# Pairs in long runs and in blocks, and a convolution in products and sums, in a routed-attention and gated-FFN kernel

## The chip, the cores and the metric

One core of a Trainium2 chip runs the whole program. The metric is device time in microseconds; each kernel is run several times and the median counts.

## The reference

Attention in which a query sees only the keys that fall to the same one of 16 centroids, then a gated FFN with a convolution over three tokens:

```python
# q, k, v: (4, 8, 768, 64) float32, centroids: (8, 16, 64)
q_assign = argmax(q_n . c_n), k_assign = argmax(k_n . c_n)      # per head, by normalized vectors
scores = where(q_assign == k_assign, q @ k.T / 8, -1e9)
attn_out = softmax(scores) @ v
x = attn_out as (4, 768, 512)
h = relu(x @ w_in)                                              # (4, 768, 1024)
conv = w[0]*h[t-1] + w[1]*h[t] + w[2]*h[t+1]                    # per channel, zero at both ends
out = (h * sigmoid(conv)) @ w_out                               # (4, 768, 512) float32
```

## The kernel before, in words

The work on attention goes by 16 pairs of heads g, four to a batch. A pair's q and k are loaded into one buffer `qk_in` (three of them, `NQK`), turned so that the head dimension lies on the partitions, cast to f16 into `ext`, and compared with the centroids (`assign`, L329; `argmax`, L356, steps M0 to M6). The centroid of each token becomes three rows that stand below the 64 rows of q and k in `ext`, so that a score is one matmul with 67 rows (`scores`, L435, step S), followed by one exponential (`exps`, L449, step E) and the product with v (`values`, L459, step V). A slot t is one pair with either its first 512 queries or its last 256; there are 32 slots with 3 or 6 steps of each kind, 144 in all.

Pairs 0 to 7 are loaded a head at a time (`load_q`, `load_k`, L268 to L274, steps LQ and LK: 768 runs of 256 bytes each) and turned by fp32 transposes on TensorE (`transposes`, L289, step T) with a copy out of PSUM (`chunk_copy`, L312, step Q). Pairs 8 to 15, named in `BLOCKS`, are loaded in quarters (`load_blocks`, L276, step LZ: 768 runs of 128 bytes each) and turned in 32x32 blocks on VectorE (`turn_blocks`, L302, step Z). For all pairs but the first, the second head is moved to the lower partitions by a copy within SBUF (`shift_pair`, L322, step CX) and the three rows are written by a transfer (`bias_rows`, L405, step BX). v is loaded by LV and cast by CV, the FFN's weights by LW and CW.

The output of attention is normalized (`reciprocals`, `normalize`, steps P and N) into `x16` and turned into `xT`, either by transposes on TensorE with a copy (`x_transposes`, `xT_copy`, steps X and Y) or by a transposing transfer (`xT_transfer`, L506, step XD).

The FFN goes by 24 units n, six to a batch: four units with two blocks of 128 channels for the first 510 tokens, two units with four blocks for the last 258. A unit is two steps of the first layer (`ffn_in`, L528, step I, 4 matmuls of 512 columns or 8 of 256), a relu into `hpad` (`relu`, L543, step R) which has columns for the neighbours on both sides, the convolution, a tanh (`tanh`, L589, step H) and the gate (`gate`, L599, step G), which writes `hg`. The second layer is `ffn_out` (L614, step O, two matmuls of 512 columns), then a copy and a store (`evac`, `store`, steps F and FX).

The convolution of 21 units is made on VectorE by `tap` (L565): per block one product of the middle tap with its weight (L572), which starts at an even column of `hpad`, and two fused products and sums (L574, steps b and c beside a). That of units 19, 22 and 23 is made on TensorE by `conv` (L576, step W, three matmuls with diagonal matrices of weights that GpSimd prepares in 24 steps `_tp`, L750), and its tanh and gate go block by block.

The order is written out by hand: `PLAN` (L26) is one list of steps, and each step issues its instructions on the engines that it names. So the order within each engine, and within SP's queue, which issues nearly all transfers, is that of the list. A transfer that waits for its data holds all that stand behind it in that queue.

## Time and profile before

| | before |
|---|---|
| time, median of 3 runs | 251.25 us |
| lowest and highest | 248.7 and 251.94 us |
| span of the profiled execution | 247.8 us, 6354 instructions |
| TensorE, VectorE, ScalarE, GpSimd busy | 229.4, 212.1, 210.1, 77.8 us |
| data moved | 35.40 MB in 97254 packets, 87537 of them under 512 bytes |

The profile is of one execution and is told by its span, from the first to the last instruction; the time of a run is taken around that and is 0.9 to 4.1 us longer. The clock that was granted to TensorE was full in all stretches but one. Busy times of groups on TensorE overlap where matmuls follow each other without a gap; the chain of waits counts each stretch once.

### The profile page before, as it was taken

To read this page: it belongs to the slowest core of one execution; us is meant where nothing else is said; L and a number is where in the kernel's file an instruction comes from. 1 tells how busy PE (TensorE), PEld (TensorE's weight loads), DVE (VectorE), ACT (ScalarE), POOL (GpSimd) and SP (SyncE) were. 2 spreads that over 40 slices of the span, in tenths; PEclk is the share of its full clock that TensorE was granted. 3 is DMA by queue.
4 is the path that set the end of the run, shared out by engine and by line. 5 is a ranking of instruction groups with operands and counts; after the bars stand their busy time and mean duration, and the time that the engine had idled before them with its cause. 6 is when DMAs were issued, how large, how long until landed. Compare 5 with 4: busy or idle time off the path is not lost.

```text
span 247.8 us, 6354 instructions
## 1 busy us (share of the span) xinstructions
PE 229.4 (93%) x2443; PEld 146.2 (59%) x2443; DVE 212.1 (86%) x484; ACT 210.1 (85%) x277; POOL 77.8 (31%) x135
## 2 busy tenths in 40 slices
PE   8698889999898699969998999999999999999994
PEld 4465556557554466745465648764657677564661
DVE  4888775899999889976999999999999997899640
ACT  5586889998998699986998999998999999974442
POOL 3312352524265100462212011540365000449600
PEclk9999999999999999997999999999999999999999
DMA  6998979998779999999987961421207022111223
GB/s 147 269 247 136 221 236 289 374 264 139 140 156 164 125 131 159 118 210 197 138 161 170 172 193 55 99 57 32 70 15 224 3 66 65 42 45 54 107 96 127
DMA packets 97254, 35.40 MB, mean 143 GB/s; under 512 B 87537, under 2 KB 91657, under 8 KB 97225
## 3 DMA queue, kind: packets, MB, share of 16 engines
q1 hardware_dynamic: 97081, 34.97, 65.1%
q8 instruction: 19, 0.31, 0.6%
q14 instruction: 10, 0.08, 0.1%
q10 hardware_dynamic: 144, 0.03, 0.1%
HBM read 23.11 MB, written 6.29 MB: 119 GB/s over the span
## 4 chain that ended last, share of the span: by engine, by line
PE 38%; DVE 23%; ACT 16%; DMA 15%; issue 4%; SPq 3%; DVEq 0%; ACTq 0%
ACT attn L454 10%; DVE cnv L574 9%; PE flex L534 9%; PE sc L440 8%; PE flex L617 7%; DMA qk_in<-in_k_dram 5%; PE sc L617 4%; PE flex L467 4%; DMA xT<-x 3%; DVE hg L605 3%; DMA ext<-spk 3%; DMA ext<-ext 2%; DMA qk_in<-in_q_dram 2%; DVE x L490 2%; PE flex L295 2%
## 5 line engine op out<-in xcount | busy, mean ns | idle before, releaser
L454 ACT ACTIVATE attn<-sc 128x1024 f16<-128x1024 f32 x144 | 141.6, 1039 | 8.0 <-PE sc L440 7.6
L440 PE MATMUL sc<-ext 67*128 67x256 f16 (+1 forms) x384 | 83.9, 328 | 2.8 <-DMA ext<-spk 1.5
L574 DVE SCALAR_TENSOR_TENSOR cnv<-hpad,cwcol,cnv 128x510 f16<-128x510 f16 (+1 forms) x108 | 68.9, 658 | 0.5
L467 PEld LDWEIGHTS <-attn 128*128 128x128 f16 x1152 | 46.3, 97 | 14.5 <-ACT attn L454 2.9
L534 PE MATMUL flex<-xT,w_in 128*128 128x512 f16 (+1 forms) x248 | 48.7, 332 | 3.8 <-DMA xT<-x 2.4
L467 PE MATMUL flex<-v,attn 128*128 128x65 f16 x1152 | 50.5, 193 | 0.2
L440 PEld LDWEIGHTS <-ext 67*128 67x128 f16 x384 | 37.4, 113 | 21.9 <-issue 6.3
L310 POOL CAST ext<-qkT 128x768 f16<-128x768 f32 (+1 forms) x31 | 29.2, 960 | 52.9 <-PE sc L440 30.1
L617 PE MATMUL flex<-w_out,hg 128*128 128x512 f16 x144 | 38.7, 378 | 0.0
L534 PEld LDWEIGHTS <-w_in 128*128 128x128 f16 x256 | 24.7, 98 | 21.2 <-issue 6.4
L605 DVE SCALAR_TENSOR_TENSOR hg<-th,hpad 128x1020 f16<-128x1020 f32 (+3 forms) x31 | 30.4, 997 | 1.2 <-ACT th L597 1.2
L617 PEld LDWEIGHTS <-hg 128*128 128x128 f16 x192 | 17.7, 97 | 17.3 <-issue 0.6
L548 ACT ACTIVATE hpad<-flex 128x512 f16<-128x512 f32 x39 | 23.1, 608 | 5.3 <-PE flex L534 4.6
L597 ACT ACTIVATE th<-cnv 128x1020 f32<-128x1020 f16 (+1 forms) x21 | 22.5, 1073 | 3.0 <-DVE cnv L574 2.7
L557 POOL COPY hf<-hpad 128x6 f16<-128x6 f16 x16 | 5.7, 360 | 56.6 <-ACT hpad L548 51.7
L750 POOL TENSOR_SCALAR taps<-id,cwcol 128x128 f16<-128x128 f16 x24 | 21.2, 899 | 0.0
L490 DVE TENSOR_TENSOR x<-flex,rec 128x256 f16<-128x256 f32 x48 | 19.7, 415 | 0.5
L310 POOL CAST v<-v_in 128x768 f16<-128x768 f32 x13 | 12.4, 955 | 22.2 <-DMA v_in<-in_v_dram 14.1
L304 DVE STREAM_TRANSPOSE qkT<-qk_in 128x384 f32<-128x384 f32 x32 | 16.8, 552 | 2.5 <-DMA qk_in<-in_k_dram 2.2
L572 DVE TENSOR_SCALAR cnv<-hpad,cwcol 128x510 f16<-128x510 f16 (+1 forms) x54 | 17.4, 344 | 1.7 <-ACT hpad L548 1.5
L295 PE MATMUL flex<-id,qk_in 128*128 128x128 f32 x96 | 14.9, 281 | 2.4 <-ACT qkT L308 0.7
L337 PE MATMUL flex<-qkT,cP 128*32 128x192 f32 x240 | 12.9, 332 | 1.9 <-DVE x L490 1.2
(86 smaller groups left out, 190.1 us busy)
## 6 DMA issues: line engine op xcount, KB each, us to landing
v_in<-in_v_dram SPq DMA_DIRECT2D x16, 384.0 KB
out_dram<-o_sb SPq DMA_DIRECT2D x24, 256.0 KB
qk_in<-in_q_dram SPq DMA_DIRECT2D x16, 192.0 KB
qk_in<-in_k_dram SPq DMA_DIRECT2D x16, 192.0 KB
qk_in<-in_q_dram SPq DMA_DIRECT2D x32, 96.0 KB
qk_in<-in_k_dram SPq DMA_DIRECT2D x32, 96.0 KB
ext<-ext SPq DMA_DIRECT2D x15, 192.0 KB
hg<-in_moe_w_in_dram SPq DMA_DIRECT2D x4, 512.0 KB
```

Source lines behind the costliest of these rows:

```text
L310: (nc.vector if name == "d" else nc.gpsimd).tensor_copy(out=to, in_=src)
L440: nc.tensor.matmul(to[:, m], lhsT=keys[:, kt], rhs=ext_b[g % NE][0:KR, h, 0, Q0[a] : Q0[a] + QN[a]], start=True, stop=True, skip_group_che ...
L454: nc.scalar.activation(to, sc[at].rearrange("p n s -> p (n s)"), AF.Exp, scale=0.125)
L467: nc.tensor.matmul(avp(at)[:, jq + (2 * h if a else 0), 0 : D + 1], lhsT=attn[t, i // 3][:, o : o + P], rhs=v16_b[g % NE][:, h, kt, 0 : D ...
L490: nc.vector.tensor_tensor(out=to, in0=src, in1=by, op=ALU.mult)
L534: nc.tensor.matmul(bank[at][:, QN[a] * f : QN[a] * (f + 1)], lhsT=w_in16[:, r, f0 + (a + 1) * p + f, :], rhs=xT[:, b % 2, r, Q0[a] : Q0[a] ...
L548: nc.scalar.activation(to, src, AF.Relu)
L574: nc.vector.scalar_tensor_tensor(out=cnv, in0=src, scalar=w, in1=cnv, op0=ALU.mult, op1=ALU.add)
L597: nc.scalar.activation(to, pre, AF.Tanh, scale=0.5)
L605: nc.vector.scalar_tensor_tensor(out=hg_b[b][:, f0 + fs.start : f0 + fs.stop, LO[a] : LO[a] + N], in0=rows_of(th_t[n], n)[:, fs], scalar=1 ...
L617: nc.tensor.matmul(bank[at][:, 0:Dm], lhsT=hg_b[b][:, fb, P * tq : P * (tq + 1)], rhs=w_out16[:, fb, :], start=(fb == 0), stop=(fb == NFB ...
L750: nc.gpsimd.tensor_scalar(out=taps16[:, fb, kk, :], in0=id16[:], scalar1=cwcol[:, fb, kk : kk + 1], scalar2=None, op0=ALU.mult)
```

## The change

The first four pairs (`SPLIT`) are loaded in long runs: k in 1536 bytes per partition, q in 1024 and 512. The tokens of these pairs then stand in another order in `ext`, and the copies, the casts, `assign`, the scores, the tiles of v and the relu of the first batch follow that order with strides. For pairs 1 to 3 one cast writes both heads' first halves, and the copy within SBUF moves half of each head. Pairs 6 and 7 join the blocks, ten in all. `qk_in` gets a fourth buffer. The convolution of all 24 units is made on VectorE, with three products per block and two sums per unit; the one on TensorE, its 24 diagonal matrices, and tanh and gate by block are gone. The x tiles of slots 4 to 7 go through TensorE. `PLAN` is new from end to end. The number of steps that differ:

| step | before | after |
|---|---|---|
| LQ + LK, whole or long loads | 32 | 23 |
| LZ, block loads; Z, block turns | 64; 32 | 80; 40 |
| T (transposes in them) | 25 (96) | 19 (72) |
| W, convolution on TensorE; _tp | 10; 24 | 0; 0 |
| plain products; fused; sums | 54; 108; 0 | 192; 0; 48 |
| H, tanh; G, gate | 31; 31 | 24; 24 |
| X, x tiles by TensorE; XD, by transfer | 8; 24 | 12; 20 |
| between the 12th and the 87th E: I, O, T | 23, 20, 10 | 18, 8, 2 |
| there: LZ, LQ + LK, LV + LW, XD | 64, 10, 17, 12 | 72, 0, 17, 8 |

The core of the diff (both lists cut to their first and last lines):

```diff
-NQK = 3
+NQK = 4
...
-BLOCKS = (8, 9, 10, 11, 12, 13, 14, 15)
+NPD = 2
+BLOCKS = (6, 7, 8, 9, 10, 11, 12, 13, 14, 15)
+SPLIT = (0, 1, 2, 3)
 
 PLAN = (
-    "_id LQ.0.0 _cent _zero _cT _k.0@0 _v.0 _v.3 _n0 _pk.3 LK.0.0 _k.1@0 _id16 _v.4 _io _k.2@0 _cw0 _pk.1 "
...
-    "O.3.5.3@2 O.3.3.0@6 FX.3.4 Fa.3.5 O.3.3.1@6 O.3.3.2@6 FX.3.5 O.3.3.3@6 Fa.3.3 FX.3.3 "
+    "_cent LK.0.0 _zero _cT _v.1 _k.0@0 _n0 _id _k.1@0 LQ.1.0 _k.2@0 _k.3@0 _k.4@0 _k.5@0 LQ.0.0.0 _k.6@0 "
...
+    "O.3.3.3@1 FX.3.5 Fa.3.3 FX.3.3 "
 )
...
+    JP = (4, J - 4)
+    JH = J // 2
...
-    def qk_part(g, x, h):
-
-        t = qk_in(g)
-        return t[:, h, :, x] if g < NBH else t[:, x, :, h]
-
-    def load_q(g, h, queue=nc.sync):
+    def load_q(g, part, h=None):
         b, h0 = batch_pair(g)
-        queue.dma_start(qk_part(g, 0, h), q[b, h0 + h].rearrange("(j p) d -> p j d", p=P))
-
-    def load_k(g, h, queue=nc.sync):
+        t = qk_in(g)[:, 0]
+        if g in SPLIT:
+            hs = heads(h)
+            j0, n = JP[0] * part, JP[part]
+            to = t.rearrange("p (h j) d -> p h (j d)", h=2)[:, hs, D * j0 : D * (j0 + n)]
+            src = q[b, h0 + hs.start : h0 + hs.stop, P * j0 : P * (j0 + n)]
+            nc.sync.dma_start(to, src.rearrange("h (p j) d -> p h (j d)", j=n))
+        else:
+            to = t.rearrange("p (j h) d -> p j h d", h=2)[:, :, part]
+            nc.sync.dma_start(to, q[b, h0 + part].rearrange("(j p) d -> p j d", p=P))
+
+    def load_k(g, h=None):
         b, h0 = batch_pair(g)
-        queue.dma_start(qk_part(g, 1, h), k[b, h0 + h].rearrange("(p j) d -> p j d", j=J))
+        t = qk_in(g)[:, 1]
+        if g in SPLIT:
+            hs = heads(h)
+            to = t.rearrange("p (h j) d -> p h (j d)", h=2)[:, hs]
+            src = k[b, h0 + hs.start : h0 + hs.stop]
+            nc.sync.dma_start(to, src.rearrange("h (p j) d -> p h (j d)", j=J))
+        else:
+            to = t.rearrange("p (j h) d -> p j h d", h=2)[:, :, h]
+            nc.sync.dma_start(to, k[b, h0 + h].rearrange("(p j) d -> p j d", j=J))
 
...
     def transposes(g, c, at):
         chunk_at[g, c] = at
-        n = 3 if g < NBH else 4
-        for i in range(n):
-            x, j = divmod(n * c + i, J)
-            blocks = qk_t[g][:, x, j].rearrange("p n d -> p (n d)")
-            nc.tensor.transpose(bank[at][:, P * i : P * (i + 1)], blocks, id128[:])
+        t = qk_t[g]
+        if g < NBH:
+            blocks = [(c % 2, J * (c // 2) + 2 * i) for i in range(JH)]
+        elif g in SPLIT:
+            blocks = [(x, J * h + 2 * i) for x in range(2) for h in range(2) for i in range(JH)]
+            blocks = [y for y in blocks if (2 if y[1] % J == 4 else y[0]) == c]
+        else:
+            blocks = [divmod(4 * c + i, J) for i in range(4)]
+            blocks = [(x, 2 * j) for x, j in blocks]
+        for i, (x, j) in enumerate(blocks):
+            rows = t[:, x, j : j + 2].rearrange("p n d -> p (n d)")
+            nc.tensor.transpose(bank[at][:, P * i : P * (i + 1)], rows, id128[:])
...
+    def halves(g):
+        return qkT[g].rearrange("p x (h u) -> p x h u", h=2)
+
     def chunk_copy(name, g, c):
-        n = 384 if g < NBH else 512
-        copy(name[1:], turned(g)[:, n * c : n * (c + 1)], bank[chunk_at[g, c]][:, 0:n])
-
-    def cast_by_head(name, g, h, x):
-        copy(name[2:], ext_b[g % NE][0:D, h, x], qkT[g][D * x : D * (x + 1), h, :])
+        at = bank[chunk_at[g, c]]
+        turned(g)
+        if g < NBH:
+            to, src = halves(g)[:, c % 2, c // 2], at[:, 0:384]
+        elif g not in SPLIT:
+            to, src = turned(g)[:, 512 * c : 512 * (c + 1)], at
+        elif c < 2:
+            to, src = halves(g)[:, c, :, 0 : 2 * P], at.rearrange("p (h u) -> p h u", h=2)
+        else:
+            to, src = halves(g)[:, :, :, 2 * P : 3 * P], at.rearrange("p (x h u) -> p x h u", x=2, h=2)
+        copy(name[1:], to, src)
+
+    def cast_by_head(name, g, h, x, e):
+        copy(name[2:], ext_b[g % NE][0:D, h, x, 384 * e : 384 * (e + 1)], halves(g)[D * e : D * (e + 1), x, h])
 
     def cast_pair(name, g, x):
-        copy(name[2:], ext_b[g % NE][:, 0, x], qkT[g][:, x, :])
+        e = ext_b[g % NE]
+        if g in SPLIT:
+            copy(name[2:], e[:, :, x, 0:384], halves(g)[:, x])
+        else:
+            copy(name[2:], e[:, 0, x], qkT[g][:, x, :])
 
     def shift_pair(g):
         e = ext_b[g % NE]
-        nc.sync.dma_start(e[0:D, 1].rearrange("d a s -> d (a s)"), e[D:P, 0].rearrange("d a s -> d (a s)"))
+        if g in SPLIT:
+            to, src = e[0:D, :, :, 384:S], e[D:P, :, :, 0:384]
+            nc.sync.dma_start(to.rearrange("d h a s -> d (h a) s"), src.rearrange("d h a s -> d (h a) s"))
+        else:
+            nc.sync.dma_start(e[0:D, 1].rearrange("d a s -> d (a s)"), e[D:P, 0].rearrange("d a s -> d (a s)"))
 
...
     def assign(g, h, at):
         sims_at[g, h] = at
-        b, h0 = batch_pair(g)
-        for x in range(2)[heads(h)]:
-            tokens = qkT[g][:, x].rearrange("p (c j t) -> p j c t", c=J, j=4)
-            w = cH[:, x] if g < NBH else cP[:, g % NPR]
-            o = 0 if h is not None else 192 * x
+        for i in range(2)[heads(h)]:
+            if g in SPLIT:
+                tokens = qkT[g].rearrange("p x (h c j t) -> p h j x c t", h=2, j=4, t=32)[:, i]
+                w = cE[:, g, i]
+            else:
+                tokens = qkT[g][:, i].rearrange("p (c j t) -> p j c t", c=J, j=4)
+                w = cP[:, g % NPR]
+            o = 0 if h is not None else 192 * i
...
+                rhs=queries(rows, a) if g in SPLIT else rows[:, Q0[a] : Q0[a] + QN[a]],
...
+                    rhs=v16_b[g % NE][:, h, 2 * (kt % JH) + kt // JH if g in SPLIT else kt, 0 : D + 1],
...
+        if b in BSPLIT:
+
+            j = JP[a] // 2
+            to = to.rearrange("p f (t j e) -> p f t j e", j=j, e=2)
+            src = src.rearrange("p f (e j t) -> p f t j e", j=j, e=2)
+            to, src = (to[:, 0], src[:, 0]) if a == 0 else (to[:, :, :, 0], src[:, :, :, 0])
...
     def tap(n, f, i):
         b, a, u, f0 = unit(n)
-        if n not in cnv_t:
-            cnv_t[n] = rot.tile([P, TH], F16, name="cnv", tag="cnv")
-        src, cnv = hpad(n)[:, f, 1 + i : 1 + i + NCV[a]], rows_of(cnv_t[n], n)[:, f]
+        if i == 1:
+            if n not in cnv_t:
+                cnv_t[n] = rot.tile([P, TH], F16, name="cnv", tag="cnv")
+            to = cnv_t[n]
+        else:
+            if (n, i) not in prd_t:
+                prd_t[n, i] = rot.tile([P, TH], F16, name="prd", tag="prd", bufs=NPD)
+            to = prd_t[n, i]
+        src = hpad(n)[:, f, 1 + i : 1 + i + NCV[a]]
         w = cwcol[:, f0 + f, i : i + 1]
-        if i == 1:
-            nc.vector.tensor_scalar(out=cnv, in0=src, scalar1=w, scalar2=None, op0=ALU.mult)
-        else:
-            nc.vector.scalar_tensor_tensor(out=cnv, in0=src, scalar=w, in1=cnv, op0=ALU.mult, op1=ALU.add)
-
-    def conv(n, f, at):
-        b, a, u, f0 = unit(n)
-        conv_at[n, f] = at
-        for i in range(3):
-            nc.tensor.matmul(
-                bank[at][:, 0 : NCV[a]],
-                lhsT=taps16[:, f0 + f, i, :],
-                rhs=hpad(n)[:, f, 1 + i : 1 + i + NCV[a]],
-                start=(i == 0),
-                stop=(i == 2),
-                skip_group_check=True,
-            )
-
-    def tanh(n, f):
-        if n not in th_t:
-            th_t[n] = rot.tile([P, TH], F32, name="th", tag="th")
-        to = rows_of(th_t[n], n)
-        if f is None:
-            pre = rows_of(cnv_t.pop(n), n)
-        else:
-            to, pre = to[:, f], bank[conv_at[n, f]][:, 0 : NCV[unit(n)[1]]]
-        nc.scalar.activation(to, pre, AF.Tanh, scale=0.5)
-
-    def gate(n, f):
+        nc.vector.tensor_scalar(out=rows_of(to, n)[:, f], in0=src, scalar1=w, scalar2=None, op0=ALU.mult)
+
+    def tap_sum(n, i):
+        a = unit(n)[1]
+        cnv = cnv_t[n][:, 0 : NF[a] * NCV[a]]
+        nc.vector.tensor_tensor(out=cnv, in0=cnv, in1=prd_t.pop((n, i))[:, 0 : NF[a] * NCV[a]], op=ALU.add)
+
+    def tanh(n):
+        th_t[n] = rot.tile([P, TH], F32, name="th", tag="th")
+        nc.scalar.activation(rows_of(th_t[n], n), rows_of(cnv_t.pop(n), n), AF.Tanh, scale=0.5)
+
+    def gate(n):
         b, a, u, f0 = unit(n)
         N = NCV[a]
-        fs = slice(0, NF[a]) if f is None else slice(f, f + 1)
         if b not in hg_b:
             hg_b[b] = rot.tile([P, NFB, S], F16, name="hg", tag="hg")
         nc.vector.scalar_tensor_tensor(
-            out=hg_b[b][:, f0 + fs.start : f0 + fs.stop, LO[a] : LO[a] + N],
-            in0=rows_of(th_t[n], n)[:, fs],
+            out=hg_b[b][:, f0 : f0 + NF[a], LO[a] : LO[a] + N],
+            in0=rows_of(th_t[n], n),
             scalar=1.0,
-            in1=hpad(n)[:, fs, 2 : 2 + N],
+            in1=hpad(n)[:, :, 2 : 2 + N],
             op0=ALU.add,
```

## Rows read from the trace of the kernel before

**Rows 1.** Busy time by stretch: us, then PE, PEld, DVE, ACT, POOL, PEclk, DMA share, GB/s.

```profile
0.00:33.00 33.00, 27.28 (x284) 17.19 (x285) 24.72 (x69) 23.12 (x33) 10.91 (x41) 1.00 0.93 204
33.00:142.00 109.00, 100.56 (x1154) 64.18 (x1153) 97.15 (x217) 98.76 (x125) 32.58 (x45) 0.98 0.96 186
142.00:221.00 79.00, 78.28 (x851) 51.46 (x850) 75.61 (x173) 75.60 (x97) 23.41 (x37) 1.00 0.27 76
221.00:247.80 26.80, 23.31 (x159) 13.41 (x157) 14.65 (x27) 12.66 (x24) 10.92 (x13) 1.00 0.24 89
sum 247.80, PE 229.43 PEld 146.23 DVE 212.15 ACT 210.13 POOL 77.82; mean PE 57.36 PEld 36.56 DVE 53.04 ACT 52.53 POOL 19.45
```

**Rows 2.** The exponentials (L454) in the first two stretches: us, ACT busy and count.

```profile
0.00:33.00 33.00, 11.87 (x12) 1.00 0.93 204
33.00:142.00 109.00, 73.75 (x75) 0.98 0.96 186
```

**Rows 3.** Transfers in the chain that ended last: start us, us, what.

```profile
15.56 6.03 DMA ext<-ext
...
97.42 4.46 DMA qk_in<-in_q_dram
...
106.46 5.06 DMA xT<-x
```

**Rows 4.** TensorE in that chain, steps without a gap.

```profile
67.24 0.44 PE flex L295 x4
...
208.93 0.86 PE flex L534 x4
...
215.09 0.86 PE flex L617 x4
215.96 0.65 PE flex L580 x3
...
233.30 0.67 PE flex L580 x6
```

**Rows 5.** Groups by shape on VectorE: busy us, mean ns, idle before.

```profile
L574 DVE SCALAR_TENSOR_TENSOR cnv<-hpad,cwcol,cnv 128x510 f16<-128x510 f16 x60 | 46.5, 786 | 0.5
...
L574 DVE SCALAR_TENSOR_TENSOR cnv<-hpad,cwcol,cnv 128x258 f16<-128x258 f16 x48 | 22.7, 498 | 0.0
...
L304 DVE STREAM_TRANSPOSE qkT<-qk_in 128x384 f32<-128x384 f32 x32 | 16.8, 552 | 2.5 <-DMA qk_in<-in_k_dram 2.2 <-DMA qk_in<-in_q_dram 0.2
...
L572 DVE TENSOR_SCALAR cnv<-hpad,cwcol 128x510 f16<-128x510 f16 x30 | 10.7, 375 | 0.9 <-ACT hpad L548 0.8
L372 DVE TENSOR_TENSOR eqq<-sim,mx 128x384 f16<-128x384 f32 x15 | 9.8, 657 | 0.1
...
L572 DVE TENSOR_SCALAR cnv<-hpad,cwcol 128x258 f16<-128x258 f16 x24 | 6.7, 306 | 0.7 <-ACT hpad L548 0.7
...
L376 DVE TENSOR_TENSOR val<-eqq,iota 128x384 f16<-128x384 f16 x15 | 6.1, 407 | 0.1
...
L550 DVE TENSOR_SCALAR hpad<-flex 128x512 f16<-128x512 f32 x8 | 5.5, 684 | 3.9 <-PE flex L534 3.2 <-PE flex L496 0.6
```

**Rows 6.** Timeline of VectorE, two products, three products, the last gate: start us, us.

```profile
143.06 0.60 DVE L572 TENSOR_SCALAR cnv<-hpad,cwcol 128x510 f16<-128x510 f16 x2
143.57 1.44 DVE L574 SCALAR_TENSOR_TENSOR cnv<-hpad,cwcol,cnv 128x510 f16<-128x510 f16 x2
144.94 0.67 DVE L572 TENSOR_SCALAR cnv<-hpad,cwcol 128x258 f16<-128x258 f16 x3
...
238.97 1.44 DVE L605 SCALAR_TENSOR_TENSOR hg<-th,hpad 128x258 f16<-128x258 f32 x4 [0.38 <-ACT th L597]
```

**Rows 7.** Busy time by stretch again, columns as in rows 1: start, weights, block loads.

```profile
0.00:5.00 5.00, 3.85 (x12) 1.55 (x12) 1.87 (x9) 2.98 (x5) 2.00 (x28) 1.00 0.58 133
5.00:13.70 8.70, 6.29 (x58) 4.29 (x58) 7.10 (x22) 4.44 (x9) 2.63 (x3) 1.00 1.09 254
...
33.00:46.00 13.00, 12.62 (x176) 7.96 (x174) 8.24 (x21) 12.70 (x15) 4.27 (x6) 1.00 0.91 299
...
90.00:115.00 25.00, 23.01 (x305) 15.01 (x302) 22.19 (x59) 21.71 (x27) 7.07 (x9) 0.93 1.02 167
```

More of the change, by code (lines that the diff above doesn't have):

```diff
@@ L211 @@
     bank = [x[:] for x in flex] + [sc[i // 2][:, i % 2, :] for i in range(4)]
-    bank16 = [x.bitcast(F16) for x in flex]
+    bank16 = [x.bitcast(F16)[:] for x in flex] + [sc[i // 2].bitcast(F16)[:, i % 2, :] for i in range(4)]
     id128 = const.tile([P, P], F32, name="id128")
@@ L216 @@
     xT = const.tile([P, 2, R, S], F16, name="xT")
-    cH = const.tile([P, 2, 2 * C], F32, name="cH")
+    cE = const.tile([P, NPR, 2, 2 * C], F32, name="cE")
     cP = const.tile([P, NPR, 2 * C], F32, name="cP")
@@ L226 @@
     scratch = const.tile([P, 1], F32, name="scratch")
-    taps16 = const.tile([P, NFB, 3, P], F16, name="taps16")
     zero = const.tile([P, 384], F16, name="zero")
@@ L381, in argmax @@
             n = 2 if h is None else 1
[L382 to L384 removed]
             if i == 5:
[L386 to L388 removed]
+                to = pack_of(g, h)[:, 1]
+                if g in SPLIT:
+                    best = mx_t[key][:, 0:G].rearrange("p (n c e) -> p n e c", c=JH, e=2)
+                    to = to.rearrange("p h a (e c) -> p (h a) e c", e=2)
+                else:
+                    best = mx_t[key][:, 0:G].rearrange("p (a j h) -> p h a j", a=2, h=2)
+                eng.tensor_scalar(out=to, in0=best, scalar1=-8.5, scalar2=SHARP, op0=ALU.add, op1=ALU.mult)
             else:
@@ L417, in rows_copy, with queries @@
         at = turn_at[g, h, x]
-        cut = (0, S // 2 if x else QN[0], S)
-        cols = slice(cut[a], cut[a + 1])
-        copy(name[2:], ext_b[g % NE][D:KR, h, x, cols], bank16[at][D:KR, cols])
+        to, src = ext_b[g % NE][D:KR, h, x], bank16[at][D:KR, 0:S]
+        if x:
+            cols = slice(S // 2 * a, S // 2 * (a + 1))
+            to, src = to[:, cols], src[:, cols]
+        else:
+            to, src = queries(to, a), queries(src, a)
+        copy(name[2:], to, src)
+    def queries(rows, a):
+        return rows.rearrange("p (e u) -> p e u", e=2)[:, :, Q0[a] // 2 : (Q0[a] + QN[a]) // 2]
     attn, x16, x_at, av_at, rec_t = {}, {}, {}, {}, {}
@@ L439, in scores @@
             keys = ext_b[g % NE][0:KR, h, 1].rearrange("p (t j) -> p j t" if g in BLOCKS else "p (j t) -> p j t", j=J)
+            rows = ext_b[g % NE][0:KR, h, 0]
             nc.tensor.matmul(
@@ L512, in xT_transfer @@
         )
-    hg_b, hfs, cnv_t, th_t, in_at, conv_at, out_at, o_t = {}, {}, {}, {}, {}, {}, {}, {}
+    BSPLIT = sorted({batch_pair(g)[0] for g in SPLIT})
+    hg_b, hfs, prd_t, cnv_t, th_t, in_at, out_at, o_t = {}, {}, {}, {}, {}, {}, {}, {}
     def unit(n):
@@ L645, in load_weights @@
         if i < 6:
-            if i % 3 == 0:
+            if i not in stage:
                 staged = rot.tile([P, NFB, S], F16, name="hg", tag="hg").bitcast(F32)
@@ L682, in setup @@
         elif name == "cT":
-            nc.vector.memset(cH[:], 0.0)
+            nc.vector.memset(cE[:], 0.0)
             nc.vector.memset(cP[:], 0.0)
@@ L709, in setup @@
             if name in ("n4", "n5"):
-                to, src = cH[rows, :, cols], turned[rows, 0]
+                to, src = cE[rows, :, :, cols], turned[rows]
             else:
@@ L747, in setup @@
             )
-        elif name == "tp":
-            fb, kk = i // 3, i % 3
-            nc.gpsimd.tensor_scalar(
-                out=taps16[:, fb, kk, :], in0=id16[:], scalar1=cwcol[:, fb, kk : kk + 1], scalar2=None, op0=ALU.mult
-            )
         else:
@@ L764, in step @@
         elif name == "LQ":
-            load_q(x[0], last)
+            load_q(*x)
         elif name == "LK":
-            load_k(x[0], last)
-        elif name == "La":
-            load_k(x[0], last, nc.scalar)
-        elif name == "Lb":
-            load_q(x[0], last, nc.scalar)
+            load_k(*x)
         elif name == "LZ":
@@ L831, in step @@
             tap(*x, "acb".index(name))
-        elif name == "W":
-            conv(*x, at)
+        elif name in ("Ua", "Ub"):
+            tap_sum(x[0], 2 * (name == "Ub"))
         elif name == "H":
-            tanh(x[0], last)
+            tanh(x[0])
         elif name == "G":
-            gate(x[0], last)
+            gate(x[0])
         elif name == "O":
@@ L843, in step @@
             store(*x)
-        elif name == "FY":
-            store(*x, nc.scalar)
         else:
```

19 lines of the change are left out of this document (6 added, 13 removed), and 248 rows, old and new, of the table PLAN.

## The prediction

> **What bounds the kernel now.** I read the page first (four engines, three of them above 80% busy), then busy time by stretch, cut at the 12th and the 87th exponential and at the last one, then the chain of waits, then the groups by shape, and last the timeline of VectorE. TensorE is the bound: 229.4 us of a span of 247.8, with 18.4 us idle; VectorE has 212.1 and ScalarE 210.1 [rows 1]. The idle time of TensorE lies 5.7 us before 33 us, 8.4 us between 33 and 142, 0.7 us between 142 and 221 and 3.5 us behind that [rows 1]. The exponentials stand 12 in the first stretch and 75 in the second [rows 2]. In the first two stretches the DMA engines are busy at a share of 0.93 and 0.96, later at 0.27 [rows 1], and the chain runs there through transfers: 6.0 us for a copy within SBUF, 4.5 us for a block load of q, 5.1 us for a transposing transfer [rows 3]. So the front is TensorE waiting for a crowded queue; the last 106 us are TensorE with nothing to wait for. What is worth time is TensorE work anywhere, and DMA work before 142 us.
>
> **The change, part by part.** *TensorE.* The ten convolution steps on TensorE go: 6 matmuls of 510 columns and 24 of 258. In the chain three of the first kind take 0.65 us and six of the second 0.67 [rows 4]: 1.3 + 2.7 = 4.0 us. Pairs 6 and 7 come as blocks, so 24 fp32 transposes go; four take 0.44 us [rows 4]: 2.6 us. Four x tiles now go through TensorE, 8 transposes in f16; no row stands for them in the chain, they cost between nothing and the 0.11 us of an fp32 one, I take 0.5 us in all. Sum: 229.4 - 4.0 - 2.6 + 0.5 = 223.3 us. The scores and the values with a new order of tokens are the same matmuls; strided operands could cost something, and I put that at 0 to 2 us and take 0, since the old transposed keys were read with a stride as well.
>
> *VectorE, convolution.* Before: 69.2 us for the 108 fused products and sums and 17.4 us for the 54 plain products [rows 5], 86.6 us for 21 of 24 units. After: all 24 units, 96 products of 510 columns, 96 of 258, and 48 sums of about 1024. A product alone has a busy time of 10.7/30 = 0.36 us and 6.7/24 = 0.28 us [rows 5]; behind another product it starts the next after 0.26 and 0.20 (two in 0.51 us until 143.57, three in 0.59 until 145.53) [rows 6]. I take 0.31 and 0.25, in the middle, because the order puts other work between them: 29.8 + 24.0 us. A sum of two f16 tensors that long is not in the trace. The fused steps grow from 0.47 us (22.7/48) at 258 columns to 0.78 (46.5/60) at 510, 1.2 ns a column; two f16 inputs of 384 columns take 0.41 us where f32 takes 0.66 [rows 5], 0.65 ns a column less, so some 0.5 ns; 0.41 us and 640 columns more of that are 0.73. From below, two plain products of 510 columns cost 2 x 0.26; from above, two fused steps 2 x 0.78. I take 0.70, since type and operation are those of the f16 row: 33.6 us. Sum 87.4 us, bounds 69 to 136; so the three units that leave TensorE come at about no cost, and VectorE changes by +0.8 (-18 to +50).
>
> *VectorE, the rest.* Eight more block turns at 16.8/32 = 0.53 us [rows 5] are +4.2 us. Gates by unit in place of single blocks, one chunk copy less, three weight casts less, and more small copies of the bias and the x tiles roughly cancel (an estimate by counts, -2 in sum). VectorE: 212.1 + 0.8 + 2.2 = about 215 us.
>
> *ScalarE and GpSimd.* ScalarE gives away copies and does the tanh in 24 instead of 31 pieces: some 6 us less of 210, off the path. GpSimd loses 24 tap matrices; it has 77.8 us in all [rows 1] and hides it either way.
>
> *DMA.* From the stretches of one kind each I make a price of 192 KB in 256-byte runs: 197 KB at 254 GB/s with a share of 1.09 is 0.85 us of all engines; a block load of 98 KB at 167 GB/s and 1.02 is 0.60 us; long runs go at 299 GB/s and 0.91 [rows 7]. A pair costs 3.4 us the old way, 4.8 us in blocks, 2.4 us in long runs. Four pairs save 4.0 us of the queue in the first stretch, two more pairs in blocks cost 2.8 us in the second. The price of an issue on SP's queue stays; 16 more block loads and 9 fewer whole loads, 4 fewer transposing transfers, each of which waits at the head of that queue for its x tile and holds all loads behind it.
>
> *Order.* Between the 12th and the 87th exponential the new list has 18 first-layer steps instead of 23, 8 second-layer steps instead of 20 and 8 chunks of transposes less. At 0.86 us for a first-layer step, 0.43 for a second-layer one and 0.11 for a transpose [rows 4] that is 4.3 + 5.2 + 3.5 = 13 us, of which seven more value steps give a little back: TensorE has some 88.5 us there instead of 100.6. The transfers in the same stretch fall by less: 72 block loads for 64 plus 10 whole ones, 8 transposing transfers for 12, 17 loads of v and weights for 17. So the queue is as crowded per us of TensorE as before. What was taken out stands behind the 87th exponential, where TensorE now has about 108 us, and VectorE, with all the convolution that went with it, some 105.
>
> *Sum of idle time.* First stretch: the chain of exponentials is as long as before and the 6 us copy meets a queue with 4 us less in it: 5.7 becomes 4.5. Second: 8.4 x 88.5 / 100.6 = 7.4, less one for the fourth buffer and the fewer transposing transfers: 6.5. Third: TensorE and VectorE equally loaded, so the one waits for the other now and then; 0.7 becomes 2.7. End: the last gate is followed by second-layer steps, one copy and one store as before: 3.5. In all 17.2, and 223.3 + 17.2 = 240.5 us of span. The page gives the profiled execution as its span; the median of the runs, 251.25, stands 3.45 us above it. 240.5 + 3.45 = 244.0 us.
>
> **A rule against it.** The products for the outer taps read hpad from columns 1 and 3, that is 2 bytes off a multiple of four; the middle tap, the only product in the trace, reads from column 2 [rows 5]. The Trainium skill, page "VectorE: DVE Perf Modes", section "Mode 2×_1P — pack two bf16 into one 32-bit read", asks for 4-byte alignment for the packed rate. Its page "Vector Engine (DVE) Microarchitecture Reference", section 5.1, says that measured chips make no difference there. No row here shows an odd start in a packed operation. By the first page the time is that of rival 2, by the second that of the sum.
>
> **Rivals.** (1) *The queue binds the second stretch.* For it: the share is 0.96 there already, the worst part of it (90 to 115 us) stands at 1.02 [rows 7], and the transfers fall less than TensorE's work. Against it: four buffers instead of three, and an emptier first stretch from which loads can run ahead. If idle time becomes 12% of that stretch, 88.5 / 0.88 gives 12.1 us in place of 6.5: 240.5 + 5.6 + 3.45 = 249.5 us: no change. (2) *The outer products run one column at a time*, the slower end. Then 64 of 510 columns cost as an unpacked product does, 0.68 us [rows 5], instead of 0.31, and 64 of 258 about 0.15 us more: +33 us, VectorE 248. To that come its idle time before 13.7 us, 3.1 + 1.6 us [rows 7], and 7.4 us behind the last gate, which ended at 240.4 [rows 6]: 260 us of span, 263.5 us. It decides from the point where VectorE and these 12 us pass 240.5, at 13 us more than I count. Against it: nothing in the trace; for it: nothing either but one rule. (3) *The idle time goes too*: the crowded queue was the cause of most of the 14 us in the first two stretches, and with it eased to 6 there, 2 and 3.5 later, the time is 223.3 + 11.5 + 3.45 = 238 us.
>
> **How the numbers follow.** Forecast 0.50 (240 to 247 us), rival 1 0.25, rival 3 0.13, rival 2 0.12. A measurement of this kernel can tell about 2% from no change, so faster means below 246.2 us and slower above 256.3. Faster: 0.46 of the forecast's half and rival 3, 0.59; within 2%: the remaining 0.04 and rival 1, 0.29; slower: rival 2, 0.12. The range goes from 235, below rival 3, to 252, above rival 1, and leaves out rival 2.
>
> **What would show it.** TensorE busy at 221 to 226 us; the new product lines with a mean near 0.3 us, the same for all three taps, and sums near 0.7; VectorE's total between 208 and 220; idle time of TensorE before the 87th exponential near 11 us. Wrong in the products: means of 0.6 for taps 0 and 2. Wrong in the queue: block loads and transposing transfers as pieces of 4 to 6 us in the chain, and over 10 us idle in the second stretch. Wrong in the order: gaps of TensorE behind the 142nd us that end at a gate or a sum.

## The result, and the profile after

The changed kernel takes 241.54 us (240.21 to 242.2, 4 runs) against 251.29 (248.7 to 251.94, 4 runs): a ratio of 0.964, 95% interval 0.958 to 0.970. The forecast was 244.0 us. The profiled execution took 240.21 us, its span is 238.4. Some executions of a kernel run slower at a lower granted clock; all ratios leave them out, the medians do not.

Busy time of the changed kernel by stretch, cut as in [rows 1] about the 12th, the 87th and the last exponential; columns as there:

```profile
0.00:29.00 29.00, 26.01 (x246) 16.65 (x247) 22.64 (x62) 22.04 (x33) 10.00 (x42) 1.00 0.79 210
29.00:124.60 95.60, 85.55 (x1110) 57.24 (x1109) 81.31 (x222) 83.85 (x96) 31.34 (x49) 0.98 1.05 184
124.60:208.80 84.20, 83.88 (x886) 55.00 (x885) 81.86 (x225) 82.14 (x106) 16.11 (x30) 1.00 0.38 95
208.80:238.40 29.60, 25.56 (x160) 13.41 (x157) 22.94 (x57) 15.80 (x26) 0.92 (x4) 1.00 0.31 117
sum 238.40, PE 221.00 PEld 142.31 DVE 208.76 ACT 203.83 POOL 58.37; mean PE 55.25 PEld 35.58 DVE 52.19 ACT 50.96 POOL 14.59
```

The length of a stretch minus its first busy time is TensorE's idle time: 2.99, 10.05, 0.32 and 4.04 us, 17.4 in all, against 18.4 before. So of the 9.4 us of span that went, 8.4 are TensorE's work (229.4 to 221.0) and 1.0 its idle time. Two things changed their place. The second stretch has a DMA share of 1.05, higher than before (0.96), and more idle time of TensorE than before. The third has none, and VectorE is now busy for 81.86 of its 84.20 us, 97%.

VectorE's groups by shape in the changed kernel, busy us, mean ns, idle before:

```profile
L628 DVE TENSOR_SCALAR prd<-hpad,cwcol 128x510 f16<-128x510 f16 x64 | 21.8, 357 | 0.3
L633 DVE TENSOR_TENSOR cnv<-cnv,prd 128x1020 f16<-128x1020 f16 x32 | 21.7, 677 | 0.0
...
L628 DVE TENSOR_SCALAR prd<-hpad,cwcol 128x258 f16<-128x258 f16 x64 | 15.8, 282 | 0.1
L633 DVE TENSOR_TENSOR cnv<-cnv,prd 128x1032 f16<-128x1032 f16 x16 | 11.0, 688 | 0.2
L628 DVE TENSOR_SCALAR cnv<-hpad,cwcol 128x510 f16<-128x510 f16 x32 | 10.7, 343 | 0.3
...
L628 DVE TENSOR_SCALAR cnv<-hpad,cwcol 128x258 f16<-128x258 f16 x32 | 8.6, 281 | 0.1
```

These are the successors of the convolution rows in [rows 5]. prd are the outer taps, which start at odd columns; cnv is the middle tap. They cost the same within 14 ns. The six rows sum to 89.6 us for 24 units; before it was 86.6 for 21.

The chain of the changed kernel that ended last, in the second stretch (start us, us, what):

```profile
66.51 0.52 SPq L287
67.08 4.04 DMA qk_in<-in_q_dram
73.20 5.71 DMA ext<-ext
78.99 4.23 DMA ext<-spk
83.26 0.65 PE sc L484 x2
...
91.91 5.85 DMA qk_in<-in_q_dram
...
107.73 2.79 DMA qk_in<-in_q_dram
111.71 3.60 DMA xT<-x
115.35 4.15 DMA xT<-x
```

The copy within SBUF (ext from ext), the loads of q and the transposing transfers are the pieces of [rows 3]. Two more kinds of piece stand beside them. SPq L287 is the issue of a block load on SP's queue: between 57.6 and 67 us the chain goes through one such issue after another, and all of them are 8.2% of the chain, as much as the loads of q themselves (8.0%). The other is ext from spk: when a pair's half is copied, its bias rows are sent, and only then can its first scores run. The waits of TensorE in the same kernel name that transfer (total us, times, longest):

```profile
PE sc L484 <- DMA ext<-spk: 7.6, 6, 2.8
```

7.4 of these 7.6 us lie in the second stretch, most of its 10 us in this execution. What the profile can't say is whether these transfers were sent too late or moved too slowly; the runs below bear on it.

### The profile page after: what moved, and what is told of

It is laid out like the page before. It is cut to its first block, busy times and chain, and to the rows that moved or that the text cites. A ratio compares the mean times of both kernels' runs of the same rounds, so it can differ in the third digit from the quotient of the medians.

```text
span 238.4 us, 6270 instructions
## 1 busy us (share of the span) xinstructions
PE 221.0 (93%) x2397; PEld 142.3 (60%) x2397; DVE 208.8 (88%) x563; ACT 203.8 (85%) x259; POOL 58.4 (24%) x124
## 2 busy tenths in 40 slices
DMA packets 93719, 35.14 MB, mean 147 GB/s; under 512 B 80353, under 2 KB 88313, under 8 KB 93689
## 4 chain that ended last, share of the span: by engine, by line
PE 40%; DMA 19%; ACT 15%; DVE 11%; SPq 10%; issue 3%; DVEq 0%; ACTq 0%
PE flex L656 11%; ACT attn L498 10%; PE sc L484 9%; SPq L287 8%; PE flex L579 8%; DMA qk_in<-in_q_dram 8%; DMA ext<-spk 5%; PE flex L511 5%; DMA xT<-x 3%; DMA ext<-ext 2%; PE sc L656 2%; ACT th L637 2%; DVE cnv L633 2%; PE flex L720 2%; DVE hg L644 2%
## 5 line engine op out<-in xcount | busy, mean ns | idle before, releaser
L484 PE MATMUL sc<-ext 67*128 67x512 f16 (+1 forms) x384 | 84.9, 329 | 8.4 <-DMA ext<-spk 7.6
L656 PE MATMUL flex<-w_out,hg 128*128 128x512 f16 x168 | 43.4, 379 | 0.1
L628 DVE TENSOR_SCALAR prd<-hpad,cwcol 128x258 f16<-128x258 f16 (+1 forms) x128 | 37.3, 319 | 0.4
L324 POOL CAST ext<-qkT 128x768 f16<-128x768 f32 (+1 forms) x31 | 25.0, 822 | 37.1 <-DVE qkT L318 27.7
L633 DVE TENSOR_TENSOR cnv<-cnv,prd 128x1020 f16<-128x1020 f16 (+1 forms) x48 | 32.7, 681 | 0.3
L644 DVE SCALAR_TENSOR_TENSOR hg<-th,hpad 128x1020 f16<-128x1020 f32 (+1 forms) x24 | 29.2, 1217 | 2.8 <-ACT th L637 2.8
L637 ACT ACTIVATE th<-cnv 128x1020 f32<-128x1020 f16 (+1 forms) x24 | 26.1, 1089 | 1.6 <-DVE rec L522 1.5
L318 DVE STREAM_TRANSPOSE qkT<-qk_in 128x384 f32<-128x384 f32 x40 | 21.5, 558 | 5.2 <-DMA qk_in<-in_q_dram 3.3
L669 ACT ACTIVATE o_sb<-flex 128x512 f32<-128x512 f32 x19 | 11.4, 610 | 6.2 <-PE flex L656 4.2
L324 POOL CAST v<-v_in 128x768 f16<-128x768 f32 x12 | 9.9, 829 | 23.3 <-DMA v_in<-in_v_dram 17.2
L309 PE MATMUL flex<-id,qk_in 128*128 128x128 f32 x72 | 11.6, 291 | 1.2 <-DVE ext L324 0.6
```

Source lines behind the costliest of these rows:

```text
L318: nc.vector.transpose(turned(g)[:, 384 * i : 384 * (i + 1)], src)
L324: (nc.vector if name == "d" else nc.gpsimd).tensor_copy(out=to, in_=src)
L484: nc.tensor.matmul(to[:, m], lhsT=keys[:, kt], rhs=queries(rows, a) if g in SPLIT else rows[:, Q0[a] : Q0[a] + QN[a]], start=True, stop=Tr ...
L628: nc.vector.tensor_scalar(out=rows_of(to, n)[:, f], in0=src, scalar1=w, scalar2=None, op0=ALU.mult)
L633: nc.vector.tensor_tensor(out=cnv, in0=cnv, in1=prd_t.pop((n, i))[:, 0 : NF[a] * NCV[a]], op=ALU.add)
L637: nc.scalar.activation(rows_of(th_t[n], n), rows_of(cnv_t.pop(n), n), AF.Tanh, scale=0.5)
```

## The experiments

All runs, medians of the runs and the ratio to the kernel before on the same chip, then three distances from each profiled execution: start to the 12th exponential, 12th to 87th, 87th to the last (144th).

| kernel | us | ratio (95%) | to 12th | 12th to 87th | 87th to last |
|---|---|---|---|---|---|
| before | 251.29 | 1 | 31.0 | 108.6 | 81.3 |
| changed | 241.54 | 0.964 (0.958 to 0.970) | 28.1 | 96.8 | 83.5 |
| fused | 257.32 | 1.024 (1.014 to 1.034) | 28.1 | 97.6 | 97.3 |
| before_conv | 259.04 | 1.035 (1.026 to 1.044) | 30.8 | 109.9 | 82.1 |
| long_blocks | 229.93 | 0.922 (0.917 to 0.928) | 27.9 | 88.1 | 83.1 |
| pool_cx_bx | 247.91 | 0.982 (0.977 to 0.987) | - | - | - |
| dummy_mid | 243.26 | 0.971 (0.963 to 0.980) | 28.1 | 99.0 | 83.3 |
| dummy_late | 245.49 | 0.978 (0.969 to 0.987) | 28.1 | 99.0 | 87.1 |
| before_long | 252.85 | 1.011 (1.007 to 1.015) | 32.9 | 109.5 | 81.0 |
| split_two | 242.77 | 0.971 (0.961 to 0.980) | 31.1 | 99.1 | 83.8 |
| nqk3 | 242.02 | 0.974 (0.967 to 0.981) | 28.1 | 98.2 | 83.9 |
| before_long4 | 250.91 | 1.009 (1.003 to 1.015) | 33.9 | 105.7 | 81.8 |
| act_bx | 249.44 | 0.995 (0.989 to 1.000) | 30.2 | 95.0 | 89.3 |
| early_cx | 241.66 | 0.966 (0.960 to 0.971) | 28.0 | 98.9 | 83.5 |

A caution first. dummy_late has the changed kernel's own program up to the 87th exponential, yet its second distance is 99.0 and not 96.8: one execution of that stretch differs from another by some 2 us. The third distance repeats within 0.8 us where the program is the same (83.1 to 83.9). Of pool_cx_bx the profiled execution took 254.6 us, 6.7 over its median, so its distances are left out.

**fused: the changed kernel with the old convolution.** One product and two fused steps per block, all 24 units on VectorE; the rest of the new order is kept, except that the middle tap of a block must come first:

```
         if i == 1:
...
-        nc.vector.tensor_scalar(out=rows_of(to, n)[:, f], in0=src, scalar1=w, scalar2=None, op0=ALU.mult)
+            nc.vector.tensor_scalar(out=cnv, in0=src, scalar1=w, scalar2=None, op0=ALU.mult)
+        else:
+            nc.vector.scalar_tensor_tensor(out=cnv, in0=src, scalar=w, in1=cnv, op0=ALU.mult, op1=ALU.add)
```

> The changed kernel with the convolution back in one product and two fused steps per block, all 24 units still on VectorE. By the rows of before and after this is some 99 us of VectorE in place of 89.6, +10 us. Theory 1 (TensorE sets the end behind the 87th exponential, VectorE follows at 97% with some 9 us idle there): most of the 6 us that fall there are absorbed, time 242 to 246 us. Theory 2 (VectorE sets that stretch): all of it is paid, 248 us or more.

257.32 us, 15.8 above the changed kernel. VectorE has only 9.6 us more (218.4 against 208.8). The two fused groups by shape, and busy time in pieces of 5 us (columns as above):

```profile
L621 DVE SCALAR_TENSOR_TENSOR cnv<-hpad,cwcol,cnv 128x510 f16<-128x510 f16 x64 | 47.0, 750 | 0.5
L621 DVE SCALAR_TENSOR_TENSOR cnv<-hpad,cwcol,cnv 128x258 f16<-128x258 f16 x64 | 28.3, 487 | 0.2
```

```profile
170.00:175.00 5.00, 2.80 (x14) 1.51 (x13) 5.00 (x11) 3.01 (x5) 0.00 (x0) 0.86 0.21 65
175.00:180.00 5.00, 5.00 (x49) 3.40 (x48) 0.04 (x1) 2.43 (x3) 0.00 (x0) 0.50 0.12 25
180.00:185.00 5.00, 2.88 (x53) 2.10 (x52) 2.50 (x4) 3.79 (x4) 0.82 (x1) 0.95 0.02 5
```

First TensorE waits while VectorE is full (2.80 of 5 us). Then its granted clock falls to 0.50, it takes a whole 5 us for what had piled up, and VectorE stands idle in turn. Up to the 87th exponential this kernel takes as long as the changed one, within the scatter; 13.8 us are lost from there to the last exponential and 3.8 behind it. So VectorE binds the third stretch too, and what is added to it there is paid more than once. The expectation that slack would take it in was wrong.

**before_conv: the old order with the new convolution.** Products and sums for all 24 units, no convolution on TensorE, the old list of steps otherwise:

```
-    taps16 = const.tile([P, NFB, 3, P], F16, name="taps16")
...
+        nc.vector.tensor_tensor(out=cnv, in0=cnv, in1=prd_t.pop((n, i))[:, 0 : NF[a] * NCV[a]], op=ALU.add)
```

> The old kernel and order with only the convolution changed: products and sums on VectorE for all 24 units, no matmuls for it and no diagonal matrices. Theory 1: TensorE has 4 us less in the last stretch, which it sets; 247 to 249 us. Theory 2 (the gain of the change comes from VectorE): VectorE stays within 1 us, so 250 to 254 us.

259.04 us, 3.5% slower than before, which no theory gave. Most of the loss lies behind the last exponential: 34.6 us instead of 26.9 before. One piece of it:

```profile
240.00:250.00 10.00, 3.59 (x8) 1.01 (x8) 8.67 (x23) 2.13 (x2) 0.00 (x0) 0.66 0.13 49
```

VectorE is at its last convolutions, TensorE has 3.59 us of work in 10, and the granted clock is 0.66 in the mean. Each part alone is thus slower than before: all the rest of the change with a convolution in fused steps by 2.4%, the new convolution in the old order by 3.5%; both together are 3.6% faster. That the new order leaves TensorE more second-layer steps to cover the last convolutions (43 behind the last exponential, 36 before) is my reading of it; it was not tried by itself. This run also takes from the last units their tanh and gate by block, which may cost some of it.

**long_blocks: the block loads read 3072-byte runs.** Same bytes, same steps; the tokens are others, so the output is not the reference's:

```
-        src = (k if x else q)[b, h0 + r // 2, :, 32 * (r % 2) : 32 * (r % 2 + 1)]
+        src = (k if x else q)[b, h0 + r // 2, 384 * (r % 2) : 384 * (r % 2 + 1), :]
...
```

> The changed kernel with the same number of block loads and the same bytes, but read in runs of 3072 bytes instead of 128 (so other tokens stand in the buffers; the output is not the reference's). Theory 1 (the many short runs of the block loads keep the DMA engines full between the 12th and the 87th exponential, and that makes the 10 us of idle TensorE there): DMA share there well below 0.8, idle 3 to 5 us, time 234 to 237 us. Theory 3 (the order and issue time on SP's queue make it, not the engines behind it): 239 to 242 us.

229.93 us, 11.6 below the changed kernel, more than expected; the spans of the two profiled executions differ by 9.2 us, 8.7 of them in the second stretch. Its second and third stretch:

```profile
27.90:116.10 88.20, 85.33 (x1129) 57.06 (x1122) 82.09 (x224) 84.04 (x98) 33.26 (x49) 1.00 0.78 204
116.10:199.20 83.10, 83.00 (x882) 54.71 (x881) 81.10 (x223) 81.64 (x106) 16.00 (x30) 1.00 0.34 94
```

TensorE does the same work (85.33 us) in 88.2 us, with 2.9 idle; the third stretch is unchanged. 34,839 packets instead of 93,719 take the DMA share from 1.05 to 0.78. The 128-byte runs of the block loads cost this kernel most of the idle time of the second stretch. But the edit eases a second thing too. The issue of the 40 block loads of k on SP's queue (ns, shortest/median/longest), in the changed kernel and here:

```profile
L287 SPq DMA_DIRECT2D qk_in<-in_k_dram x40: 423/530/1562, 25.8 to 136.0; - x40
```

```profile
L287 SPq DMA_DIRECT2D qk_in<-in_k_dram x40: 324/422/1424, 25.4 to 126.8; - x40
```

SP spends 91% of the second stretch issuing transfers in the changed kernel and 78% here, so this run alone doesn't exclude theory 3. Two runs below help: in split_two SP issues for 70% of that stretch and in act_bx for 78%, at DMA shares of 0.97 and 1.03. Their second stretches:

```profile
31.10:130.20 99.10, 92.61 (x1153) 61.49 (x1147) 82.75 (x219) 85.95 (x99) 32.63 (x47) 0.95 0.97 170
```

```profile
30.20:125.20 95.00, 86.44 (x1129) 57.93 (x1117) 81.83 (x224) 84.60 (x97) 31.88 (x47) 0.98 1.03 179
```

Their second distances, 99.1 and 95.0, are near the changed kernel's 96.8 and not near 88.1. So a lighter queue on SP doesn't give these 8.7 us by itself; that the engines behind it do is the better supported reading, though no run changes them alone.

**dummy_mid and dummy_late: work added to TensorE.** Thirty matmuls on a zero tile that nothing reads, one name for each in the list of steps, in the second or in the third stretch:

```
+_k.99@1
 I.0.0@1
```

> The changed kernel with 30 matmuls of 384 columns more (about 0.16 us each, 4.8 us of TensorE in all), spread between the 14th and the 87th exponential; nothing reads what they write. Theory 1 (in this stretch the transfers set the pace and TensorE has some 10 us of slack; behind the 87th exponential TensorE and VectorE together set it): at most 2 us longer, 241.5 to 243.5 us. Theory 2 (TensorE's work counts everywhere, its idle time is only how the order happens to fall): 4 to 6 us longer, 245.5 to 247.5 us.

> The changed kernel with the same 30 matmuls of 384 columns (some 4.8 us of TensorE), now spread between the 90th and the 143rd exponential. Theory 1 (TensorE is 99.6% busy there): the whole of it, 4 to 6 us longer, 245.5 to 247.5 us. Theory 3 (VectorE alone sets that stretch, and TensorE only looks busy since it waits inside its work): at most 2 us longer, 241.5 to 243.5 us.

243.26 and 245.49 us: 1.7 and 4.0 above the changed kernel (the intervals overlap; the stretches are clearer). dummy_mid from the 28.1st to the 126th us, dummy_late from the 125th to the 214th:

```profile
28.10:126.00 97.90, 91.26 (x1151) 60.98 (x1144) 83.89 (x219) 84.68 (x97) 34.52 (x49) 0.97 1.07 181
```

```profile
125.00:214.00 89.00, 89.00 (x935) 58.89 (x934) 83.13 (x230) 84.88 (x108) 16.17 (x30) 1.00 0.35 90
```

TensorE's total grows by 5.6 us in dummy_mid (226.6), and its second stretch is as long as dummy_late's, which has none of that work there: most of it lies in the idle time, 6.6 us in the window above for 10.05 in the changed kernel. In the third TensorE is busy in every microsecond, and the distance from the 87th to the last exponential grows by 3.6 us. With fused this says that both engines bind the third stretch, as theory 1 had it, and theory 3 falls.

**before_long and before_long4: the long runs alone.** The old kernel, pairs 0 to 3 loaded in 1536-byte runs; then with a fourth q/k buffer too:

```
-        queue.dma_start(qk_part(g, 0, h), q[b, h0 + h].rearrange("(j p) d -> p j d", p=P))
+        if g < 4:
+            queue.dma_start(qk_slot(g, h), q[b, h0 + h].rearrange("(p j) d -> p (j d)", j=J))
...
-NQK = 3
+NQK = 4
```

> The kernel before with one thing changed: the q and k loads of pairs 0 to 3 read runs of 1536 bytes (the tokens then stand in other places, so the output is not the reference's). 6,144 packets less at the front. Theory 1 (the transfers set the pace up to the 87th exponential): the 24th exponential 2 to 4 us earlier, and 1 to 3 us of it kept at the end: 248 to 250 us against 251.3. Theory 2 (the front's gain is taken back by the block loads that come behind and by TensorE's own work): the early exponentials come earlier, the 87th does not, and the time is within 1 us of the kernel before.

> The kernel before with the loads of pairs 0 to 3 in runs of 1536 bytes, as in the run of that name, and four q/k buffers in place of three (output not the reference's). Theory 1 (in that run the SP queue stood behind loads that waited for a buffer, so the bytes came no earlier): the 24th exponential at 45 us or before, 247 to 250 us in all. Rival (the order of the old kernel's steps, not the buffers, decides when the early exponentials run): 251 to 254 us, as with three buffers.

252.85 and 250.91 us, both some 1% slower than before. The first stretch of before_long:

```profile
0.00:33.00 33.00, 27.76 (x276) 17.66 (x276) 23.68 (x68) 21.91 (x32) 9.53 (x40) 0.95 0.66 192
```

Against the first of [rows 1] the DMA share has fallen from 0.93 to 0.66, and the 12th exponential comes at 32.9 us, not 31.0. In the old order the start is not bound by the amount that the queue must move. The 24th, which the expectations name, comes 3 us later in both runs (47.9 us for 44.9). So theory 1 fell for this stretch, theory 2 has its early part wrong, and more buffers did not mend it (250.91 us lies between the two ranges of before_long4). What gives the changed kernel its 28.1 us must be in the order of its steps or in what it does with these pairs behind the load (one cast for both heads, half the copy within SBUF); no run here tried these alone.

**nqk3: three buffers in the changed kernel.**

```
-NQK = 4
+NQK = 3
```

> The changed kernel with three q/k buffers in place of four, nothing else. The load of a pair then waits until the pair three before it has been turned, and what stands behind it on SP's queue waits too. Theory 1 (the loads must run far ahead, since the transfers set the pace up to the 87th exponential): 243 to 248 us, lost before the 87th exponential. Rival (the fourth buffer is only spare, a load is issued early enough with three): 241 to 242.5 us.

242.02 us, as the rival said. The intervals of the two ratios overlap only just (0.967 to 0.981 and 0.958 to 0.970), so the 1% between 0.974 and 0.964 is not clear of the noise: the fourth buffer is worth little or nothing.

**split_two: four more pairs in long runs.** Pairs 4 to 7 are added to the long runs, eight pairs stay in blocks; TensorE's six bank transposes with a copy each take the place of eight turns:

```
-BLOCKS = (6, 7, 8, 9, 10, 11, 12, 13, 14, 15)
-SPLIT = (0, 1, 2, 3)
+BLOCKS = (8, 9, 10, 11, 12, 13, 14, 15)
+SPLIT = (0, 1, 2, 3, 4, 5, 6, 7)
```

> The changed kernel with pairs 4 to 7 loaded in the long runs too (SPLIT 0 to 7, eight pairs in blocks in place of ten): some 12,000 packets less up to the 87th exponential; TensorE gets six bank transposes of 4 x 128 columns and gives nothing back (+2.6 us), VectorE has 8 block turns less and 4 copies more (about -1 us). Theory 1 (the transfers set the pace there): by the price of the run with long block loads (11.6 us for 59,000 packets) 2.4 us shorter, TensorE's 2.6 us lie in its slack: 238 to 241 us. Theory 2 (TensorE's work counts everywhere): 243 to 245 us.

242.77 us, between the two expectations. It starts badly: the 12th exponential comes 3 us later, and its chain shows why.

```profile
23.86 5.10 DMA qk_in<-in_q_dram
29.01 1.12 PE flex L307 x4
30.12 0.85 PE sc L482 x2
```

A load of q takes 5.10 us to land, TensorE waits for it, and in the profiled execution, at 245.57 us the longest of four, these 3 us are never won back. With 78,935 packets the second distance (99.1) is no shorter. So theory 1's price per packet does not hold for this version; whether its start or TensorE's added transposes spoil it (TensorE is busy for 92.6 us there, for 85.6 in the changed kernel, at a granted clock of 0.95 for 0.98) stays open.

**pool_cx_bx and act_bx: another engine sends the small transfers.** The copies between halves and the bias rows from GpSimd's queue; the bias rows from ScalarE's (queue=nc.scalar):

```
...
-    def bias_rows(g, queue=nc.sync):
+    def bias_rows(g, queue=nc.gpsimd):
```

> The changed kernel with the copies within SBUF and the bias rows issued by GpSimd's queue instead of SP's, so that they don't stand behind the block loads. If their wait behind loads on one queue is the price: the 4 to 6 us pieces for them in the chain shrink, idle TensorE in the middle 10 to 6 us, time 237 to 239 us. If the engines are shared in any case: 241 to 243 us. If GpSimd's issue is slow or held up: 244 us or more.

> The changed kernel with the bias transfers (15 of 18 KB, read by every first scores matmul) issued from ScalarE's queue in place of SP's. Theory 1 (in the middle TensorE waits for transfers that stand behind 80 block loads on SP's queue): TensorE's waits for the bias transfers shrink to under half, 238 to 240.5 us. Rival (the transfer's own 4 to 5 us among short packets are what is waited for, and ScalarE pays for the issue): 241.5 to 245 us.

By their ratios, 0.982 and 0.995 for 0.964, both are slower than the changed kernel; the first as its third condition said, the second by more than either of its expectations. On GpSimd the issue waits in that engine's order, with the casts behind it. Of the bias transfers in the profiled execution of pool_cx_bx, GpSimd's idle time before 7 of the 15 issues (us, times), and the time to landing of all:

```profile
  DVE spk L324: 19.6, 7
...
DMA to landing us min/median/max: 2.5/4.4/6.5
```

On ScalarE, the chain of act_bx behind the 87th exponential, where it loses 5.8 us (89.3 for 83.5), and busy time there:

```profile
126.91 5.20 DMA ext<-spk
132.16 0.71 PE sc L484 x2
```

```profile
130.00:135.00 5.00, 3.42 (x14) 1.44 (x12) 1.88 (x5) 2.84 (x4) 0.00 (x0) 0.76 0.80 148
```

18 KB take 4.4 us in the median of pool_cx_bx and 5.20 in this piece of act_bx, no less than the 5.12, 4.23 and 3.10 us of the pieces in the changed kernel's chain. That fits engines that are shared. The Trainium skill, page "Trainium Kernel Development and Optimization", section "Key Constraints", says just this: queues of several engines run on the same 16 DMA engines, and only the time to issue is saved. The landing times agree with it. The issues did go out sooner behind the copy that makes the rows (2.6 us in the median in the changed kernel, 1.4 in act_bx, 0.3 in pool_cx_bx), and the time got worse: on GpSimd the wait before the issue holds up that engine's casts; what ScalarE pays was not traced further.

**early_cx: the same small transfers sent earlier.** Casts, copies between halves and bias rows up to 60 steps earlier, nothing added:

```
+CX.6
 ...
-CX.6
```

> The changed kernel with the casts of q and k (pairs 6, 7, 8, 10, 12, 13, 15), the transfers between halves (pairs 6 to 15) and the bias transfers (most of pairs 4 to 13) put up to 60 steps earlier in the order, nothing else; no work added or taken away. Theory 1, in the narrow form (what TensorE waits for before the 87th exponential is the chain cast, half transfer, bias transfer, first scores): its 7.6 us of waits for the bias transfer fall to under 4 us, and 2 to 4 us of the time go, 237.5 to 240 us. Rival (the 16 transfer engines are full there, so what is sent earlier only makes the block loads land later, and those are then waited for): 240.5 to 243 us, with TensorE's idle time before the 87th exponential at 9 us or more.

241.66 us, as the rival said. TensorE's waits for the bias rows, and the second stretch:

```profile
PE sc L483 <- DMA ext<-spk: 3.1, 3, 1.5
```

```profile
28.00:126.90 98.90, 90.45 (x1128) 59.41 (x1121) 84.54 (x224) 85.31 (x97) 34.72 (x50) 0.95 1.05 182
```

The wait that the profile named reads 3.1 us instead of 7.6 and the time stays: 8.5 us idle, a granted clock of 0.95, and the DMA share is 1.05 again. But that the edit cut this wait is not shown. In dummy_late, whose program is the changed kernel's up to the 87th exponential, the same wait (line 485 there) is shorter still:

```profile
PE sc L485 <- DMA ext<-spk: 2.4, 2, 1.3
```

Which transfer TensorE is found waiting for changes from one execution to the next, and the stretch takes 97 to 99 us each time. Only longer runs shortened it by clearly more than that scatter. No version here beats the changed kernel with the reference's output.

## Why the prediction was right

The sum was 223.3 us of TensorE's work and 17.2 idle; it became 221.0 and 17.4. The 3.45 us put on top came out as 3.1. For one and the same execution the time stands only 1.8 us above the span (240.21 and 238.4); the rest is that the profiled execution was the shortest of the four. The 0.9 to 4.1 us told of the kernel before mix executions in the same way; in its later runs the distance is 2.1 us (250.24 and 248.1). By the steps of the sum:

- *TensorE.* Work fell by 8.4 us where I had 6.1. By groups, the convolution's three sum to 5.2 us where I had 4.0, the transposes gave 3.3 (14.9 to 11.6) where I had 2.6, and the x tiles cost 1.3 (2.5 to 3.8) where I had 0.5. No other kind of step changed by more than 1.6 us; groups overlap, so these don't add up to the total.
- *"TensorE work anywhere" is worth time.* This step does not hold for the second stretch of the changed kernel: dummy_mid puts 30 matmuls there for 1.7 us, dummy_late the same 30 behind it for 4.0. The total comes out even so: work taken out of that stretch turns into idle time there, and the sum counts both.
- *VectorE, convolution.* 89.6 us for 87.4. Busy time by count gives products at 0.34 and 0.25 us where I took 0.31 and 0.25, sums at 0.68 where I took 0.70. The lower bound (69) and the upper (136) were both far off; f16 row and type were the right neighbour.
- *VectorE, the rest.* 208.8 us for about 215. The other groups grew by 2.6 where I had 2.2. But I added up groups, and groups overlap: before they sum to 22.7 us more than VectorE's total, after to 31.7. A product begins some 0.08 us before the one ahead ends ([rows 6]: at 143.57 us, where the pair ahead ends at 143.66), and the convolution now has 240 instructions for 162. The sum left that out.
- *Idle time.* That 17.4 stands for 17.2 is luck: the second stretch is 3.5 us over, the first and third are 1.5 and 2.4 under. First stretch 3.0 where I had 4.5, and not for the reason given: before_long shows that, in the old order, an emptier queue does not bring the early exponentials forward. Second 10.05 where I had 6.5: the start of rival 1, whose sign (over 10 us idle, block loads of 4 to 6 us in the chain) came true, though not its size (12.1); long_blocks shows that the short runs on that queue make this idle time. The 1 us that I gave the fourth buffer and the fewer transposing transfers does not appear; for the buffer nqk3 finds nothing that is clear of the noise. Third 0.3 where I had 2.7: TensorE is never late there although VectorE is 97% busy. fused shows how near it is: 9.6 us more on VectorE and the time is slower than before.
- *Rival 2* is excluded. Outer taps cost 357 and 282 ns, the middle one 343 and 281. The Trainium skill's page "Vector Engine (DVE) Microarchitecture Reference", section 5.1, says that 4-byte alignment makes no difference, and the trace agrees within these 14 ns; the alignment that the Trainium skill's page "VectorE: DVE Perf Modes" asks for was not needed for this form. The deciding point of rival 2, 13 us more VectorE than counted, can be set beside fused: some 10 us more than measured were enough to lose all of the gain.
- *Rival 3* (idle time goes too) did not come, since the queue of the second stretch was not eased. long_blocks is that rival made real, at 229.9 us, with 10.9 us idle in all where the rival had 11.5.
- *Order.* I put 88.5 us of TensorE's work between the 12th and the 87th exponential and it has some 86 (85.55 in the window above). The step holds. before_conv shows that the new convolution alone does not gain; that it is the order that it lacks, and not another part of the change, is argued and not shown.

## What to carry to other kernels

Before a wait that the profile names is attacked, ask whether the transfer was late or the resource behind it is full, and whether another execution of the same program shows the same wait: sending the named transfer earlier moved no time, while longer runs for the same bytes took 11.6 us off. Work that goes to VectorE is paid more than once where TensorE has nothing to cover it: with TensorE at 99.6% and VectorE at 97% in the third stretch, each microsecond added to VectorE cost more than one and a half. And a right total can stand on wrong terms, so test the terms.
